# Fourier mixing and a gated feed-forward on one core: a new order of loads and weight conversions ahead of the first chunk

## The chip, the cores and the metric

The kernel runs on one core of one Trainium2 chip. The metric is the device time of one launch in microseconds. The kernel before takes 2041.99 us, the median of 8 runs (2037.69 to 2045.06). One more execution was recorded by the profiler: 2041.35 us, of which the recorded span is 2039.6 us.

## What is computed

Eight sequences x of 3008 rows and 256 features go through a two-dimensional Fourier transform of which the real part is kept, and the result through a gated feed-forward with 1536 inner features. Cut to what matters, the reference is:

```
X = np.fft.fft(x, axis=1)                 # x: (8, 3008, 256) float32
X = np.fft.fft(X, axis=2).real            # 24064 rows of 256
gate = 1 / (1 + exp(-(X @ w_gate)))       # w_gate, w_val: 256 x 1536
out  = (gate * (X @ w_val)) @ w_out       # w_out: 1536 x 256
```

The three weights arrive as 64-bit floats, and the kernel itself turns them into 32-bit ones.

## The kernel before, in words

**Sequence transform.** A batch of x is loaded into the tile x4 as 126 partitions x 4 groups x 6 rows x 256 features: for each row number s it holds the rows s, -s, M+s and M-s, with M = 1504. `fold_ops` (L218) adds and subtracts these groups in place: `point` and `first` (L222 to L227) add a row and its mirror image, `across` (L235) adds or subtracts rows half a sequence apart, and `feat` (L229) folds features j and 256-j. TensorE then multiplies the folded x with tables of cosines and sines (tile st, 126 x 2 x 6 x 753). `half` (L271) makes one such group: its `sums` are six matmuls, one for each of the six rows q, each written into PSUM bank ev or od and each shown in the trace as two pieces of 376 or 377 columns; its `then` evacuates them, with a ScalarE copy (L283) and two VectorE operations (L287, L290). A batch has six groups: four with cosines, into pk and ek, and two with sines, into qk.

**Feed-forward.** The feature transform is merged into the gate and value weights: `weight_use` calls `merge` (L190), eight TensorE pieces `ps` from the table dt and a weight piece, two ScalarE copies into G1 and G2 (L197, L198) and two tiny transfers ge<-G (L200). Output weights go to `forms` (L203), which makes seven sums of blocks on ScalarE and GpSimd. The main loop runs over 8 batches x 6 chunks of 256 sequence frequencies x 6 pairs of feature tiles; each pair takes two turns i of the loop at the bottom of the kernel. A turn calls `front` (matmuls pa and pb, then VectorE L350 twice, L353, L354), `gate` for the turn before (VectorE L365, GpSimd L367 or L369 to L371), from the fifth turn on `back` (the matmuls po), the weight steps in `pre`, the sigmoid (ScalarE L573), and whatever stands in `side` for that turn.

**Weights.** There are 18 pieces, numbered j in `jobs` (L124), each 128 x 2 x 256 values of 8 bytes, 512 KB. Piece j goes through `weight_load` (L130, a transfer on SP's queue), `weight_parts` (L161, two ScalarE operations, L166 and L167), `weight_join` (L169, three VectorE operations L176, L177, L179 and one GpSimd addition L181) and `weight_use`. A piece that is loaded before the main loop lands in buffers that later serve other ends (z, pk, qk, ek, c7); pieces from `KEEP` on use the tile mega, which stands where x4 of batch 0 stood and so is loaded when the sine matmuls have read x4.

**What sets the order.** The schedule is written by hand: each engine executes its instructions in the order in which the code issues them, and loads go through SP's queue in program order. Before the main loop (L469 to L508) that order is:

- SP's queue: three times (a third of x, a third of the cosine table), weights 0 and 1, the sine table in thirds, weights 2 to 7, and after the sine sums weights 8 to 10. dt is issued by ScalarE.
- fold of batch 0 in three parts of two q each; after each part two rows q of all four cosine groups.
- conversions 0 and 1 between the cosine evacuations; merges 0 and 1 between the sine sums; conversions 2 and 3 ahead of the sine evacuations, 4 after them.

In the loop `weight_step` (L520) spreads conversions 5 to 17 over the turns: first one and then two, alternately. Batches 1 to 7 of x are loaded by the same `load_x` during the batch before.

Of the kernel before, what the change touches and what calls it, by code (L numbers as in the profile page):

```python
# [7 lines left out]
F32 = mybir.dt.float32  # L8
# [37 lines left out]
def kernel(  # L46
# [53 lines left out]

    X = {}

    def load_x(b, nq):
        X[b] = xp.tile([NP, 4, NQ, D], F32, name="x4", tag="x4")
        return [lambda q=q: nc.sync.dma_start(out=X[b][:, :, q : q + nq], in_=xf[b, :, :, q : q + nq])
                for q in range(0, NQ, nq)]

    dt = const.tile([P, 2, D], F32, name="dt")
    st = const.tile([NP, 2, NQ, NE + NO], F32, name="st")
# [6 lines left out]
    ed = dram.tile([B - 1, NK], F32, name="ed")  # L116

    def load_table(t, nq):
        return [lambda q=q: nc.sync.dma_start(out=st[:, t, q : q + nq], in_=stab[:, t, q : q + nq])
                for q in range(0, NQ, nq)]  # L120

    jobs = [(w, c - (w == 2)) for c in range(NPR + 1) for w in range(3)  # L124
            if (c if w == 2 else c < NPR)]
    RAW, WS = {}, {}
    mega = []
    KEEP = 8

    def weight_load(j):  # L130


        w, c = jobs[j]
        src = (moe_w_gate, moe_w_val, moe_w_out)[w]
        src = src[2 * c * P : 2 * (c + 1) * P, :] if w == 2 else src[:, c * WC : (c + 1) * WC]
        src = src.rearrange("(c p) f -> p c f", p=P)
        if j < 6:
            if j < 3:
                raw = zp.tile([P, 2, WC, 2], I32, name="raw", tag="z")
            else:  # L140
                raw = pqp.tile([P, 2, WC, 2], I32, name="raw", tag=("pk", "qk", "ek")[j - 3])
            ws = (app if j < 3 else hp).tile([P, 2, WC], F32, name="ws", tag="ae" if j < 3 else "h")
        else:
            if j < KEEP:
                both = cp.tile([P, 3, 2 * WC], F32, name="both", tag="c7")
                r, i = 0, 2
            else:
                if not mega:
                    mega.append(xp.tile([P, 12, 2 * WC], F32, name="mega", tag="x4"))
                both, r, i = mega[0], (j - KEEP) % 3 * 2, 6 + (j - KEEP) % 6  # L150
            raw = both[:, r : r + 2].rearrange("p a n -> p (a n)").bitcast(I32).rearrange(
                "p (c f w) -> p c f w", c=2, w=2)
            ws = both[:, i].rearrange("p (c f) -> p c f", c=2)
        WS[j] = ws
        if src.dtype == F32:
            nc.sync.dma_start(out=ws, in_=src)
        else:
            RAW[j] = raw
            nc.sync.dma_start(out=raw.rearrange("p c f w -> p c (f w)"), in_=src.bitcast(I32))

    def weight_parts(j):  # L161

        if j in RAW:
            raw, ws = RAW[j], WS[j]
            lo, hi = raw[:, :, :, 0], raw[:, :, :, 1]
            nc.scalar.activation(ws, hi.bitcast(F32), AF.Abs)  # L166
            nc.scalar.activation(lo, lo.bitcast(U32), AF.Copy, scale=2.0 ** -29)  # L167
# [50 lines left out]
    def fold_ops(b, nq):  # L218
        x4 = X.pop(b)
        ops = []  # L220

        def point(e, i, j, q):  # L222
            e.tensor_tensor(x4[:, i, q, 1:D], x4[:, i, q, 1:D], x4[:, j, q, D - 1 : 0 : -1],  # L223
                            op=ALU.add)

        def first(e, i, j, q):
            e.tensor_tensor(x4[:, i, q, 0], x4[:, i, q, 0], x4[:, j, q, 0], op=ALU.add)  # L227

        def feat(e, v, r, q):  # L229
            e.memset(r[:, q, 0:1], 0.0)  # L230
            e.tensor_tensor(r[:, q, 1:HD], v[:, q, 1:HD], v[:, q, D - 1 : HD : -1],  # L231
                            op=ALU.subtract)
            e.tensor_tensor(v[:, q, 1:HD], v[:, q, 1:HD], v[:, q, D - 1 : HD : -1], op=ALU.add)  # L233

        def across(e, blk, q):  # L235
            e.tensor_tensor(parts[blk][0][:, q], x4[:, 0, q], x4[:, 2, q],
                            op=(ALU.add, ALU.subtract)[blk])

        parts = [(x4[:, 1], x4[:, 3]), (x4[:, 0], x4[:, 2])]
        qs = [slice(q, q + nq) for q in range(0, NQ, nq)]  # L240
        pool = nc.gpsimd
        if b:

            for i in (0, 2):
                ops += [lambda i=i, q=q: point(pool, i, i + 1, q) for q in qs]
                ops.append(lambda i=i: first(pool, i, i + 1, slice(0, NQ)))
            for blk in range(2):
                ops += [lambda blk=blk, q=q: across(pool, blk, q) for q in qs]
            for v, r in parts:
                ops += [lambda v=v, r=r, q=q: feat(pool, v, r, q) for q in qs]  # L250
        else:

            def part(q, es):
                for e, i in zip(es, (0, 2)):
                    point(e, i, i + 1, q)
                    first(e, i, i + 1, q)
                across(es[0], 0, q)
                feat(es[0], *parts[0], q)
                across(es[1], 1, q)
                feat(es[1], *parts[1], q)  # L260
            for n, q in enumerate(qs):
                ops.append(lambda q=q, es=(nc.vector, pool if n else nc.vector): part(q, es))
        for blk, (v, r) in enumerate(parts):
            W[b, blk] = (v[:, :, 0:HD], r[:, :, 0:HD],
                         v[:, :, HD : HD + 1].to_broadcast([NP, NQ, P]))
        return ops
# [31 lines left out]
    def seq_start(b):  # L298
        PQE[b] = (pqp.tile([P, NK], F32, name="pk", tag="pk"),
                  pqp.tile([P, NK], F32, name="qk", tag="qk"),  # L300
                  pqp.tile([P, NK], F32, name="ek", tag="ek"))
        if b:
            nc.sync.dma_start(out=PQE[b][2], in_=ed[b - 1 : b, :].to_broadcast([P, NK]))
# [163 lines left out]


    nc.scalar.dma_start(out=dt, in_=dtab.rearrange("(c p) d -> p c d", p=P))  # L469
    for fx, ft in zip(load_x(0, 2), load_table(0, 2)):  # L470
        fx()
        ft()
    for j in range(2):
        weight_load(j)
    for f in load_table(1, 2):
        f()
    for j in range(2, KEEP):
        weight_load(j)
    seq_start(0)
    cos = [seq_group(0, blk, what, (2 * blk, 2 * blk + 1) if what else None)  # L480
           for blk in range(2) for what in (0, 2)]
    for i, f in enumerate(fold_ops(0, 2)):
        f()
        for sums, _ in cos:
            sums(2 * i, 2 * i + 1)
    weight_parts(0)
    cos[0][1]()()
    weight_parts(1)
    weight_join(0)
    cos[1][1]()()  # L490
    cos[2][1]()()
    weight_join(1)
    cos[3][1]()()
    sin = [seq_group(0, blk, 1) for blk in range(2)]
    for i in range(NQ // 2):
        for sums, _ in sin:
            sums(2 * i, 2 * i + 1)
        if i < 2:
            weight_use(i, i)
    for j in range(2, 4):  # L500
        weight_parts(j)
        weight_join(j)
    for _, then in sin:
        then()()
    weight_parts(4)
    weight_join(4)
    for j in range(KEEP, KEEP + 3):
        weight_load(j)  # L508

    per = 2 * NPR * len(chunks)  # L510
    side = {}

    def at(i, *fs):
        side.setdefault(i, []).extend(fs)
# [2 lines left out]

        at(i, lambda: at(i + 1, f(*args)))

    def weight_step(i, *js):  # L520

        for j in js:
            pre.setdefault(i, []).append(lambda j=j: weight_parts(j))
            at(i, lambda j=j: weight_join(j))
            if KEEP <= j < len(jobs) - 3:
                at(i, lambda j=j: weight_load(j + 3))

    pre = {}
    for c in range(1, NPR + 1):
        i, j = 2 * c - 3, 3 * c - 1  # L530
        if c < NPR:
            at(max(i, 0), lambda j=j: weight_use(j))
            at(i + 1, lambda j=j: weight_use(j + 1))
            at(i + 2, lambda j=j: weight_use(j + 2))
        else:
            at(i, lambda j=j: weight_use(j))
        if c == NPR:
            weight_step(i - 1, j)
        elif c > 1:
            weight_step(i - 1, j)  # L540
            weight_step(i, j + 1, j + 2)
    i0 = 2 * NPR
    at(i0 + 1, lambda: [f() for f in load_x(1, 3)], e_load)

    for b in range(B - 1):
        s0 = b * per
        if b:
            at(s0 + 1, lambda b=b: [f() for f in load_x(b + 1, 3)])
        f0, g0, gs = (s0 + 9, s0 + 36, 8) if b else (i0 + 9, i0 + 36, 7)

        def folds(f0=f0, b=b):
            for j, f in enumerate(fold_ops(b + 1, 2)):
                at(f0 + j, f)
        at(f0 - 1, folds)
        at(g0 - 3, lambda b=b: seq_start(b + 1))
        for j in range(4):
            split(g0 + gs * j, lambda b=b, j=j: whole(*seq_group(b + 1, j // 2, j % 2)))
# [78 lines left out]
```

## Time and profile before

| What | Value |
|---|---|
| median of 8 runs | 2041.99 us |
| the profiled execution, its own time | 2041.35 us |
| its span | 2039.6 us |
| TensorE busy (matmul) | 2000.3 us, 98% |
| VectorE busy | 1752.2 us, 86% |
| GpSimd busy | 1334.7 us, 65% |
| ScalarE busy | 498.7 us, 24% |
| transfer engines, mean | 35 GB/s |

How to read it: times in the trace count from the span's start. A row of the timeline gives start, duration, engine, line, operation, out<-in, shape, and in brackets how long the engine was idle before it and what released it. A row of the stages gives the length of the stretch, the busy time of each engine with its number of instructions, the granted clock of TensorE (1.00 is full), the busy share of the 16 transfer engines and what they moved. "SPq" is the queue that SP issues transfers on. The first turn of the main loop stands at about 50 us: its first pa matmul starts at 49.76 us.

### The profile page before, as it was taken

The numbers are of one execution on the slowest core, as the hardware profiler recorded it, in microseconds if no ns is written. First come the engines' busy times: TensorE is split into PE (matmuls) and PEld (weight loads), VectorE is DVE, ScalarE is ACT, GpSimd is POOL, SyncE is SP. The second block draws the span as 40 slices with busy tenths as digits, with TensorE's granted clock in tenths as the row PEclk, the third lists the DMA queues.
The fourth block names the chain that finished last, engine by engine and source line by source line (L and its number), as shares of the span: only waits on it lengthen the run. The fifth ranks groups of instructions, "written<-read, shape, count | busy, mean of one in ns | idle before, by whom it ended". The sixth has DMA issues, their size and how long they took to land.

```text
span 2039.6 us, 27360 instructions
## 1 busy us (share of the span) xinstructions
PE 2000.3 (98%) x9168; PEld 1740.7 (85%) x9168; DVE 1752.2 (86%) x3228; ACT 498.7 (24%) x875; POOL 1334.7 (65%) x1681
## 2 busy tenths in 40 slices
PE   6899999999999999999999999999999999999998
PEld 3688789888898889988898888988889888898888
DVE  4999778988799878998789988899878988798887
ACT  2522222222222222222222222222222222222222
POOL 2678645885569755697557955589446885565665
PEclk9899999999999999999999999999999999999999
DMA  9240002010021000200012000201002010000001
GB/s 250 84 73 20 27 11 72 15 31 11 11 77 30 11 11 11 81 26 11 11 23 69 26 12 20 72 10 31 16 11 72 15 31 11 11 16 16 11 16 26
DMA packets 143162, 70.98 MB, mean 35 GB/s; under 512 B 127931, under 2 KB 128187, under 8 KB 143022
## 3 DMA queue, kind: packets, MB, share of 16 engines
q1 hardware_dynamic: 141200, 68.69, 13.0%
q8 instruction: 74, 1.21, 0.2%
q10 hardware_dynamic: 1822, 0.54, 0.1%
q14 instruction: 66, 0.54, 0.1%
HBM read 44.50 MB, written 24.68 MB: 34 GB/s over the span
## 4 chain that ended last, share of the span: by engine, by line
PE 84%; DVE 8%; POOL 4%; DMA 1%; issue 1%; SPq 1%; ACT 0%; DVEq 0%; ACTq 0%; POOLq 0%
PE po L93 37%; PE pa L93 21%; PE pb L93 20%; PE ev L93 3%; PE od L93 3%; DVE ae L350 2%; DVE h L365 2%; DVE z L354 1%; DMA st<-in_stab_dram 1%; DVE z L353 1%; POOL x L233 1%; POOL x L231 1%; POOL sf L370 1%; POOL sf L369 1%; DVE os L412 0%
## 5 line engine op out<-in xcount | busy, mean ns | idle before, releaser
L573 ACT ACTIVATE z<-z 128x512 f32<-128x512 f32 (+1 forms) x576 | 358.5, 622 | 1309.8 <-DVE z L354 1309.8
L350 DVE SCALAR_TENSOR_TENSOR ae<-ek,ge,pa 128x256 f32<-128x256 f32 (+1 forms) x1152 | 489.5, 466 | 189.0 <-PE pa L93 185.1
L93 PE MATMUL pa<-pk,G 128*128 128x256 f32 (+1 forms) x2304 | 583.3, 376 | 2.3 <-ACT a L283 2.3
L93 PE MATMUL pb<-qk,G 128*128 128x256 f32 (+1 forms) x2304 | 582.3, 375 | 1.4 <-DVE qk L287 1.4
L93 PE MATMUL po<-sf,wf 128*128 128x256 f32 (+1 forms) x2304 | 537.2, 375 | 0.8
L93 PEld LDWEIGHTS pa<-pk,G 128*128 128x128 f32 x2304 | 438.5, 190 | 60.1 <-ACT a L283 2.9
L93 PEld LDWEIGHTS po<-sf,wf 128*128 128x128 f32 x2304 | 436.2, 190 | 55.7 <-POOL sf L371 4.5
L93 PEld LDWEIGHTS pb<-qk,G 128*128 128x128 f32 x2304 | 438.2, 190 | 51.9 <-DVE qk L287 2.1
L369 POOL TENSOR_TENSOR sf<-h 128x256 f32<-128x256 f32 (+1 forms) x288 | 213.2, 740 | 391.9 <-DVE h L365 391.9
L365 DVE TENSOR_TENSOR h<-z 128x512 f32<-128x512 f32 (+1 forms) x576 | 451.6, 784 | 0.0
L353 DVE TENSOR_TENSOR z<-ae,pb 128x512 f32<-128x512 f32 (+1 forms) x576 | 390.1, 677 | 62.4 <-DVE ae L350 3.2
L93 PE MATMUL po<-h,wf 128*128 128x256 f32 (+1 forms) x1728 | 412.5, 375 | 0.0
L354 DVE TENSOR_TENSOR z<-ae,pb 128x512 f32<-128x512 f32 (+1 forms) x576 | 386.0, 670 | 0.0
L93 PEld LDWEIGHTS po<-h,wf 128*128 128x128 f32 x1728 | 328.3, 190 | 37.1
L367 POOL TENSOR_TENSOR sf<-h 128x256 f32<-128x256 f32 (+1 forms) x288 | 219.2, 761 | 213.0 <-DVE h L365 209.3
L370 POOL TENSOR_TENSOR sf<-sf,h 128x256 f32<-128x256 f32 (+1 forms) x288 | 215.3, 747 | 22.6
L371 POOL TENSOR_TENSOR sf<-h,sf 128x256 f32<-128x256 f32 (+1 forms) x288 | 214.6, 745 | 22.6
L93 PE MATMUL ev<-st,x 126*128 126x377 f32 (+3 forms) x216 | 78.2, 488 | 17.5 <-DMA st<-in_stab_dram 13.6
L452 ACT COPY c<-po 128x512 f32<-128x512 f32 (+1 forms) x141 | 76.9, 580 | 64.0 <-PE po L93 63.9
L412 DVE STREAM_TRANSPOSE os<-c 128x256 f32<-128x256 f32 x192 | 83.9, 437 | 0.2
L93 PE MATMUL od<-st,x 126*128 126x377 f32 (+3 forms) x216 | 77.5, 485 | 0.0
L223 POOL TENSOR_TENSOR x<-x 126x510 f32<-126x510 f32 x44 | 63.0, 1432 | 19.7 <-DMA x<-in_xf_dram 19.7
(83 smaller groups left out, 727.3 us busy)
## 6 DMA issues: line engine op xcount, KB each, us to landing
x<-in_xf_dram SPq DMA_DIRECT2D x14, 1512.0 KB
out_dram<-os SPq DMA_DIRECT2D x288, 64.0 KB
ek<-ed SPq DMA_DIRECT2D x7, 752.5 KB
out_dram<-os SPq DMA_DIRECT2D x92, 56.0 KB
st<-in_stab_dram SPq DMA_DIRECT2D x6, 741.2 KB
x<-in_xf_dram SPq DMA_DIRECT2D x3, 1008.0 KB
mega<-in_moe_w_out_dram SPq DMA_DIRECT2D x4, 512.0 KB
raw<-in_moe_w_gate_dram SPq DMA_DIRECT2D x3, 512.0 KB
```

The lines of the kernel that those rows point to most:

```text
L93: nc.tensor.matmul(o, l, r, start=start, stop=stop, skip_group_check=True)
L350: nc.vector.scalar_tensor_tensor(out=ae[:, g], in0=ek[:, ks], scalar=ge[:, g, f : f + 1], in1=pa[:, g], op0=ALU.mult, op1=ALU.add)
L353: nc.vector.tensor_tensor(z[:, :, 0], ae, pb, op=ALU.add)
L354: nc.vector.tensor_tensor(z[:, :, 1, ::-1], ae, pb, op=ALU.subtract)
L365: nc.vector.tensor_tensor(h[:, fh], z[:, 0], z[:, 1], op=ALU.mult)
L367: tt(s[:, 2], h[:, 0, 0], h[:, 0, 1], op=ALU.subtract)
L369: tt(s[:, 0], h[:, 0, 1], h[:, 1, 1], op=ALU.add)
L370: tt(s[:, 1], s[:, 0], h[:, 0, 0], op=ALU.subtract)
L371: tt(s[:, 3], h[:, 1, 0], s[:, 1], op=ALU.subtract)
L412: nc.vector.transpose(os_[:, s, 0:nb, h, :], t[:, slot, 0 : nb * TB])
L452: nc.scalar.copy(t[:, 2 * j : 2 * j + 2, 0:n], PO[j][:, :, 0:n])
L573: nc.scalar.activation(z[:, 0], z[:, 0], AF.Sigmoid)
```

## The change

- `load_x` loads a batch as two transfers, groups 0 and 1 and then groups 2 and 3, each with all six rows (12 KB in a row per partition), for every batch. Before, batch 0 came in thirds (2 KB in a row) and the others in halves by q (3 KB in a row).
- The cosine table comes in two transfers (9 KB in a row), the sine table in one (18 KB in a row).
- SP's order becomes: weights 0 and 1, x, cosine table, weights 2 to 5, sine table, weights 6 to 9; after the sine sums weights 10 to 12. `KEEP` is 10, so two more pieces are loaded before the loop, in the buffers os and sf.
- Conversions and merges 0 and 1 stand ahead of everything else on ScalarE, VectorE, GpSimd and TensorE.
- Batch 0 is folded in two parts of three q. VectorE adds groups 0 and 1 for both, GpSimd adds groups 2 and 3 for the second; then `half1` is all on VectorE and `half2` on VectorE and GpSimd. After each part three rows q of all four cosine groups follow; then both sine groups.
- All evacuations stand behind these sums in the code: conversions 2 to 4 ahead of the first, 5 ahead of the second, 6 and 7 ahead of the first sine evacuation, 8 ahead of the last. Merge 2 stands directly ahead of the loop.
- In the loop turn i converts piece i+9 (turns 0 to 8, one each) and the uses follow at fixed turns.

The diff, cut to its core:

```
-    def load_x(b, nq):
-        return [lambda q=q: nc.sync.dma_start(out=X[b][:, :, q : q + nq], in_=xf[b, :, :, q : q + nq])
-                for q in range(0, NQ, nq)]
+    def load_x(b):
+        for h in range(0, 4, 2):
+            nc.sync.dma_start(out=X[b][:, h : h + 2], in_=xf[b, :, h : h + 2])
...
-    KEEP = 8
+    KEEP = 10
...
+            def half1(q):
+                point(nc.vector, 2, 3, q)
+                first(nc.vector, 2, 3, q)
+                for blk in range(2):
+                    across(nc.vector, blk, q)
+                    feat(nc.vector, *parts[blk], q)
+            def half2(q):
+                across(nc.vector, 0, q)
+                feat(nc.vector, *parts[0], q)
+                across(pool, 1, q)
+                feat(pool, *parts[1], q)
+            for q in qs:
+                point(nc.vector, 0, 1, q)
+            first(nc.vector, 0, 1, slice(0, NQ))
+            point(pool, 2, 3, qs[1])
+            first(pool, 2, 3, qs[1])
+            ops += [lambda: half1(qs[0]), lambda: half2(qs[1])]
...
     for j in range(2):
         weight_load(j)
-    for f in load_table(1, 2):
-        f()
-    for j in range(2, KEEP):
-        weight_load(j)
+    load_x(0)
+    load_table(0, NQ // 2)
+    for j in range(2, 6):
+        weight_load(j)
+    load_table(1, NQ)
+    for j in range(6, KEEP):
+        weight_load(j)
...
+    weight_parts(0)
+    weight_parts(1)
+    weight_join(0)
+    weight_join(1)
+    weight_use(0)
+    weight_use(1)
     seq_start(0)
...
-    for i, f in enumerate(fold_ops(0, 2)):
+    for i, f in enumerate(fold_ops(0, NQ // 2)):
         f()
         for sums, _ in cos:
-            sums(2 * i, 2 * i + 1)
+            sums(*range(i * NQ // 2, (i + 1) * NQ // 2))
...
+    for sums, _ in sin:
+        sums(*range(NQ))
+    evacuate = [then for _, then in cos + sin]
+    for then, js in zip(evacuate, ((2, 3, 4), (5,), (), (), (6, 7), (8,))):
+        weight_round(*js)
         then()()
...
     for j in range(KEEP, KEEP + 3):
         weight_load(j)
+    weight_use(2)
...
     pre = {}
+    for j in range(9, len(jobs)):
+        pre.setdefault(j - 9, []).append(lambda j=j: weight_parts(j))
+        at(j - 9, lambda j=j: weight_join(j))
+        if KEEP <= j < len(jobs) - 3:
+            at(j - 9, lambda j=j: weight_load(j + 3))
+    for j in range(3, len(jobs)):
+        w, c = jobs[j]
+        at(2 * c + (-3, -2, 1)[w], lambda j=j: weight_use(j))
```

`weight_round(*js)` calls `weight_parts` and `weight_join` for each j.

More of the change, by code (lines that the diff above doesn't have):

```diff
@@ L118, in load_table @@
     def load_table(t, nq):
-        return [lambda q=q: nc.sync.dma_start(out=st[:, t, q : q + nq], in_=stab[:, t, q : q + nq])
-                for q in range(0, NQ, nq)]
+        for q in range(0, NQ, nq):
+            nc.sync.dma_start(out=st[:, t, q : q + nq], in_=stab[:, t, q : q + nq])
     jobs = [(w, c - (w == 2)) for c in range(NPR + 1) for w in range(3)
@@ L126 @@
     RAW, WS = {}, {}
-    mega = []
-    KEEP = 8
+    shared = {}
+    KEEP = 10
     def weight_load(j):
@@ L136, in weight_load, with some @@
         src = src.rearrange("(c p) f -> p c f", p=P)
-        if j < 6:
-            if j < 3:
-                raw = zp.tile([P, 2, WC, 2], I32, name="raw", tag="z")
-            else:
-                raw = pqp.tile([P, 2, WC, 2], I32, name="raw", tag=("pk", "qk", "ek")[j - 3])
-            ws = (app if j < 3 else hp).tile([P, 2, WC], F32, name="ws", tag="ae" if j < 3 else "h")
-        else:
[L144 to L150, printed above, removed]
+        def some(n, pool, tag):
+            key = tag, (j - 6) // 3 if tag == "c7" else 0
+            if key not in shared:
+                shared[key] = pool.tile([P, n, 2 * WC], F32, name=f"w{tag}", tag=tag)
+            return shared[key]
+        if j < KEEP:
+            pool, tag = ((zp, "z"), (pqp, ("pk", "qk", "ek")[j % 3]), (op, "os"), (sp, "sf"))[
+                j // 3 if j < 6 else j // 2 - 1]
+            raw = pool.tile([P, 2, WC, 2], I32, name="raw", tag=tag)
+            if j < 6:
+                pool, tag = ((app, "ae"), (hp, "h"))[j // 3]
+                ws = pool.tile([P, 2, WC], F32, name="ws", tag=tag)
+            else:
+                ws = some(3, cp, "c7")[:, (j - 6) % 3].rearrange("p (c f) -> p c f", c=2)
+        else:
+            both = some(12, xp, "x4")
+            r, i = (j - KEEP) % 3 * 2, 6 + (j - KEEP) % 6
             raw = both[:, r : r + 2].rearrange("p a n -> p (a n)").bitcast(I32).rearrange(
@@ L251, in fold_ops @@
         else:
[L253 to L262, printed above, removed]
+            def half1(q):
[15 more added lines that the diff above has]
+            ops += [lambda: half1(qs[0]), lambda: half2(qs[1])]
         for blk, (v, r) in enumerate(parts):
@@ L469, with weight_round @@
     nc.scalar.dma_start(out=dt, in_=dtab.rearrange("(c p) d -> p c d", p=P))
-    for fx, ft in zip(load_x(0, 2), load_table(0, 2)):
-        fx()
-        ft()
     for j in range(2):
         weight_load(j)
-    for f in load_table(1, 2):
-        f()
-    for j in range(2, KEEP):
+    load_x(0)
+    load_table(0, NQ // 2)
+    for j in range(2, 6):
         weight_load(j)
+    load_table(1, NQ)
+    for j in range(6, KEEP):
+        weight_load(j)
+    def weight_round(*js):
+        for j in js:
+            weight_parts(j)
+            weight_join(j)
+    weight_parts(0)
[4 more added lines that the diff above has]
+    weight_use(1)
     seq_start(0)
@@ L481 @@
            for blk in range(2) for what in (0, 2)]
-    for i, f in enumerate(fold_ops(0, 2)):
+    for i, f in enumerate(fold_ops(0, NQ // 2)):
         f()
         for sums, _ in cos:
-            sums(2 * i, 2 * i + 1)
[L486 to L493, printed above, removed]
-    sin = [seq_group(0, blk, 1) for blk in range(2)]
[L495 to L503, printed above, removed]
+            sums(*range(i * NQ // 2, (i + 1) * NQ // 2))
+    sin = [seq_group(0, blk, 1) for blk in range(2)]
+    for sums, _ in sin:
[3 more added lines that the diff above has]
+        weight_round(*js)
         then()()
-    weight_parts(4)
-    weight_join(4)
     for j in range(KEEP, KEEP + 3):
         weight_load(j)
+    weight_use(2)
     per = 2 * NPR * len(chunks)
@@ L518, in split @@
         at(i, lambda: at(i + 1, f(*args)))
[L520 to L526, printed above, removed]
-    pre = {}
[L529 to L541, printed above, removed]
+    pre = {}
+    for j in range(9, len(jobs)):
[6 more added lines that the diff above has]
+        at(2 * c + (-3, -2, 1)[w], lambda j=j: weight_use(j))
     i0 = 2 * NPR
-    at(i0 + 1, lambda: [f() for f in load_x(1, 3)], e_load)
+    at(i0 + 1, lambda: load_x(1), e_load)
     for b in range(B - 1):
@@ L547 @@
         if b:
-            at(s0 + 1, lambda b=b: [f() for f in load_x(b + 1, 3)])
+            at(s0 + 1, lambda b=b: load_x(b + 1))
         f0, g0, gs = (s0 + 9, s0 + 36, 8) if b else (i0 + 9, i0 + 36, 7)
```

## The prediction

> **What bounds the kernel now.** I read the page first, then the busy times by stage, then the timeline of TensorE and of VectorE at the end of the ramp, then the first rows that wait for loads.
>
> ```profile
> span 2039.6 us, 27360 instructions
> ...
> PE 2000.3 (98%) x9168; PEld 1740.7 (85%) x9168; DVE 1752.2 (86%) x3228; ACT 498.7 (24%) x875; POOL 1334.7 (65%) x1681
> ...
> PE   6899999999999999999999999999999999999998
> ```
>
> TensorE is at 90% or more in 37 slices, and short only in the first two and the last. By stage:
>
> ```profile
> core 0: us, PE busy (x) PEld busy (x) DVE busy (x) ACT busy (x) POOL busy (x), PEclk, DMA share, GB/s
> 0.00:13.25 13.25, 0.00 (x1) 0.03 (x1) 3.31 (x9) 1.28 (x1) 0.20 (x4) 1.00 0.79 220
> 13.25:49.76 36.51, 29.99 (x88) 17.68 (x88) 18.36 (x35) 8.09 (x18) 12.77 (x15) 1.00 0.94 257
> 49.76:80.00 30.24, 24.34 (x86) 19.27 (x86) 26.67 (x46) 17.05 (x36) 18.40 (x20) 0.78 0.20 64
> 80.00:110.00 30.00, 24.56 (x109) 20.37 (x110) 29.00 (x47) 14.59 (x31) 25.32 (x28) 1.00 0.36 106
> 110.00:130.00 20.00, 20.00 (x95) 17.60 (x94) 18.41 (x34) 5.18 (x12) 14.23 (x21) 1.00 0.47 150
> ```
>
> TensorE idles 13.3 + 6.5 + 5.9 + 5.4 = 31 us before 110, and from there on it is full. So the end is set by when TensorE becomes full and how far it has then come; all that the change can move lies in the first 110 us. Until 49.76 the transfers bind (share 0.79 to 0.94), from 80 to 110 VectorE does (29.0 of 30.0): weight conversions stand on its queue beside the loop's own work. The last idle time, and what follows it:
>
> ```profile
> 106.36 1.99 PE L93 MATMUL ps<-mega,dt 128*128 128x256 f32 x8 [1.19 <-POOL mega L181]
> 108.19 1.03 PE L93 MATMUL pa<-pk,G 128*128 128x256 f32 x4
> 109.06 1.03 PE L93 MATMUL pb<-qk,G 128*128 128x256 f32 x4
> ```
>
> The pb matmul at 109.06 belongs to turn 9, counted from 0, and nothing holds TensorE after it. I use it as the mark: the gain is how much earlier it starts, since the matmuls behind it are the same.
>
> **A turn of the ramp, now and then.** VectorE's ae (L350) of turn 0 starts at 55.09 and that of turn 9 at 110.37, 55.3 us later, with thirteen conversions between. From turn 3 (73.80) to turn 9 it takes 36.57 us for six turns and nine conversions. A turn without a conversion takes 2.8 us (110.37 to 113.14), so a conversion costs (36.57 - 6 x 2.8) / 9 = 2.2 us, a turn with one 5.0. The rows of turn 8, where the conversion's third operation took 1.10 us, give 5.28:
>
> ```profile
> 105.09 0.86 DVE L350 SCALAR_TENSOR_TENSOR ae<-ek,ge,pa 128x256 f32<-128x256 f32 x2
> ...
> 110.37 0.86 DVE L350 SCALAR_TENSOR_TENSOR ae<-ek,ge,pa 128x256 f32<-128x256 f32 x2
> ```
>
> After the change conversions 9 to 17 stand one in each of turns 0 to 8. The mark needs the PSUM bank that ae of turn 8 frees, so it starts 8 x 5.0 - 0.6 (turn 0 has no L365) + 0.9 (that ae) = 40.3 us after ae of turn 0. With 5.28 it is 42.2; I take 5.0, a mean of six turns. TensorE has no more than that to do: nine turns at 1.73 (pa and pb), nine merges at 1.73, backs in turns 4 to 8 of 7.3, together 38.5 us. GpSimd was busy 41.7 of the 55.3 us and loses four additions of 1.4. Both stay under VectorE, though TensorE needs 5.0 of each 5.0 us from turn 4 on.
>
> **The loads.** Where engines first wait shows when they land:
>
> ```profile
> 9.85 0.69 DVE L223 TENSOR_TENSOR x<-x 126x510 f32<-126x510 f32 x1 [9.85 <-DMA x<-in_xf_dram]
> 13.25 0.97 PE L93 MATMUL ev<-st,x 126*128 126x377 f32 x1 [13.25 <-DMA st<-in_stab_dram]
> 18.14 0.69 DVE L223 TENSOR_TENSOR x<-x 126x510 f32<-126x510 f32 x1 [3.70 <-DMA x<-in_xf_dram]
> 25.96 0.69 DVE L223 TENSOR_TENSOR x<-x 126x510 f32<-126x510 f32 x1 [3.27 <-DMA x<-in_xf_dram]
> 36.20 0.56 PE L93 MATMUL ev<-st,x 126*128 126x377 f32 x1 [0.31 <-DMA st<-in_stab_dram]
> ```
>
> A third of x with a third of a table (1.79 MB) takes 8.05 us, 222 GB/s: about 4.85 for x (211 GB/s, 2 KB in a row) and 3.2 for the table (237, 6 KB). dt and the first third of x (1.29 MB) at 222 would need 5.8 of the 9.85 us, so 4.0 are fixed: issue, first bytes, last bytes.
>
> What longer rows are worth isn't shown here. In the Trainium skill, "DMA: Bandwidth & Descriptors", section Specifications, a transfer reaches line rate from pieces of 512 B on; 2 KB are beyond that, so by this rule x stays at 211 GB/s and needs 14.7 us. The rows differ: x of batch 1, 3 KB in a row, crossed while the stretch from 120.0 to 130.5 moved 287 GB/s. That stretch has no table beside it, so the stage may matter as well as the length. Ends for x: 211 to 287; I take 270, 5.7 us for each half, nearer the row of the same tensor. Tables stay at the 237 of 6 KB (9 and 18 KB are only longer), the sine table at the 262 GB/s of the stretch 25.96 to 36.20. A weight piece (0.52 MB) takes 1.8 us at the 292 GB/s of the stretch 36.2 to 48.
>
> Landing in the new order: dt 1.2 and weight 0 at 7.0, weight 1 at 8.8, x at 14.5 and 20.2, cosines at 25.0 and 29.8, weights 2 to 5 at 31.6, 33.4, 35.2, 37.0, sines at 45.7, weights 6 to 9 at 47.5, 49.3, 51.1, 52.9. The four weights cost the sine table 7.2 us; that is the price of this order on SP's queue.
>
> **The work up to turn 0.**
> - Conversions and merges 0, 1: at 7 to 16, on engines that wait for x; cost nothing. Their cover is the 11 us until x.
> - Fold: x at 20.2, then GpSimd's `point` over three rows, 1.77 x 1.5 = 2.65; VectorE's small `first` ended only with it at 18.74 (1.23 us instead of 0.15), so I let it wait again. Then `across` 1.03 and `feat` 1.3: first matmul at 25.4. `half2` ends near 32 on GpSimd, before TensorE wants it.
> - Cosines: 48 pieces of 0.317 are 15.2; the first 5.6 us of matmuls in this trace (13.25 to 18.8) ran at half pace, which costs 2.8: end at 43.4.
> - Conversions 2 to 5: landed by 37.0, VectorE needs 1.6 each, done near 39; the cosine evacuations queued behind them wait for the matmuls anyway. Cost nothing, but if weight 4 were late they would hold the banks that the sine groups need.
> - Sines: at 45.7, after 2.3 us of idle TensorE. In the trace 2.26 us of idleness (47.50 to 49.76) stand ahead of a stretch at clock 0.50 until about 55; the 2.51 us ahead of 82.00 do not. The skill, "TensorE: Matmul & The Clock Gate", What's actually happening, asks for an idle window of some 3.4 us, which would keep this gap warm. By the rule 0, by the first row 3.0 us; two rows disagree, so I take 1.5. 24 pieces are 7.6: end at 54.9.
> - Conversions 6 to 8: weight 8 at 51.1, ScalarE 1.3, VectorE behind it done at 53.4: 1.5 us ahead of the last evacuation that is queued behind it on both. If that cover is gone, each us late is a us of the end.
> - Turn 0: merge 2 (1.73) and pa (0.86) follow the sines, while ScalarE (0.5) and VectorE (1.1) evacuate: ae starts at 57.6. It was 55.09.
> - ge transfers: ae of turn 6 waited for one (1.90 us). Now they are issued a turn ahead, but in turns 2 and 4 behind a weight load that waits for GpSimd's addition: 1.4 + 0.5 + 1.2 + 1.9 = 5.0 us, one turn. Between 0 and 2 us; I take 0. Loading x of later batches in two other halves lies under a full TensorE: 0.
>
> The mark comes at 57.6 + 40.3 = 97.9 instead of 109.06: 11.2 us earlier. Span 2039.6 - 11.2 = 2028.4; this execution took 1.75 more than its span, and the median is 0.6 above it: about 2030.
>
> **Rivals.**
> - Longer rows do little: x at 211 (+3.3), the sines start cold (+1.5), perhaps turns of 5.28 (+1.9). Gain 4 to 7, 2035 to 2038. For it: the skill's rule and the tables' 237 GB/s at 6 KB. Against: 287 for x. 0.17.
> - Everything crosses at 287: x ends at 19.5, cosine sums at 42.7, sines land before that, no cold start; sines end near 50.4. Gain 16, about 2026. 0.10.
> - The conversions only move: all unfavourable ends together, with weights landing 2.26 us apart (ScalarE's waits end at 30.65 and 32.91) so that weight 8 holds the last evacuation. Gain about 2, 2040. 0.09.
> - Slower: few long rows, 126 of them to spread over 16 engines, cross worse than short ones, and the sine table, behind four weights, holds turn 0. At 160 GB/s x takes 8.0 more, cosines 4.6, sines 5.5: 18 - 11 = 7 slower, 2048. It decides from 181 GB/s down; the lowest row is 211. 0.08.
>
> **Numbers.** The forecast, 2024 to 2034, has 0.56. About 0.2% (4 us) is what a measurement of this kernel can tell from no change. Faster 0.56 + 0.17 + 0.10 = 0.83, same 0.09, slower 0.08. The range reaches from the faster case into all of the second one: 2022 to 2038.
>
> **What would show it.** Sine matmuls near 45.7, ae of turn 0 near 57.6, turns of 5.0 us with TensorE idle under 1 us in each, the mark near 98, and no idle time after it. Wrong if the sines land after 50, if VectorE waits for a ge transfer or a conversion in turns 1 to 8, or if the clock column shows half pace in turn 0 or later.

## The result, and the profile after

The changed kernel took 2029.18 us (median of 12 runs, 2026.67 to 2032.24), the kernel before beside it 2040.08 us (33 runs, 2034.03 to 2045.91): a ratio of 0.9948, with a 95% interval of 0.9937 to 0.9960. It is 10.9 us faster. The forecast was 2030.0. Beside the later runs the kernel before had medians of 2036.66, 2037.36 and 2040.19 us, so the gain is 7 to 11 us depending on which of them is taken, and ratios from different sets can differ by 0.2% where the times do not.

The page of the changed kernel, its head and the row of TensorE in 40 slices:

```profile
span 2026.9 us, 27347 instructions
...
PE 1995.8 (98%) x9168; PEld 1738.9 (86%) x9168; DVE 1755.2 (87%) x3221; ACT 498.4 (25%) x875; POOL 1328.1 (66%) x1675
...
PE   6999999999999999999999999999999999999998
```

TensorE has the same 9168 matmuls. The second slice has filled, from 8 to 9. The same five stages as before, with the same columns:

```profile
0.00:13.25 13.25, 3.83 (x10) 3.16 (x11) 5.03 (x7) 3.92 (x6) 2.77 (x6) 1.00 0.80 286
13.25:49.76 36.51, 25.76 (x74) 15.04 (x74) 27.42 (x44) 11.92 (x23) 13.74 (x11) 0.86 0.88 257
49.76:80.00 30.24, 28.00 (x126) 23.48 (x125) 27.28 (x48) 16.13 (x35) 18.46 (x22) 1.00 0.33 105
80.00:110.00 30.00, 29.70 (x137) 25.32 (x136) 28.05 (x48) 12.01 (x29) 22.81 (x31) 1.00 0.15 36
110.00:130.00 20.00, 20.00 (x95) 17.60 (x94) 19.27 (x36) 6.12 (x11) 14.44 (x21) 1.00 0.71 157
```

Read the matmul counts: in the third stage 126 instead of 86, in the fourth 137 instead of 109. TensorE's idle time there fell from 5.9 and 5.4 us to 2.2 and 0.3, and no clock below 1.00 is left behind 49.76. The second stage holds fewer matmuls than before (74 for 88), because the first cosine sum now waits for all of x. VectorE does 9 us more there; the conversions taken out of the ramp are among it.

The ends of the ramp, on the timelines of VectorE (ae of turn 0) and TensorE (pb of turn 9, the mark), each row with its start and its duration:

```profile
54.23 0.87 DVE L364 SCALAR_TENSOR_TENSOR ae<-ek,ge,pa 128x256 f32<-128x256 f32 x2 [0.77 <-PE pa L93]
```

```profile
95.17 1.03 PE L93 MATMUL pa<-pk,G 128*128 128x256 f32 x4
96.03 1.03 PE L93 MATMUL pb<-qk,G 128*128 128x256 f32 x4
```

From ae of turn 0 to the mark it takes 41.80 us, where it was 109.06 - 55.09 = 53.97. From the mark to the end it takes 2026.9 - 96.03 = 1930.9, where it was 1930.5. So the gain of this execution, 13.0 us at the mark, is 12.2 in the ramp and 0.9 ahead of it. The medians differ by 1.7 us less than these two executions do (2041.35 and 2028.71), well within the spread of either kernel's runs.

The first rows that wait for loads, on the timelines of VectorE (x) and TensorE (tables):

```profile
12.40 1.82 DVE L229 TENSOR_TENSOR x<-x 126x765 f32<-126x765 f32 x2 [1.57 <-DMA x<-in_xf_dram]
18.55 0.96 DVE L229 TENSOR_TENSOR x<-x 126x765 f32<-126x765 f32 x1 [4.24 <-DMA x<-in_xf_dram]
19.43 1.77 DVE L233 TENSOR_TENSOR x<-x 126x3 f32<-126x3 f32 x1
```

```profile
24.02 2.85 PE L93 MATMUL ev<-st,x 126*128 126x377 f32 x4 [9.27 <-DMA st<-in_stab_dram]
43.77 2.14 PE L93 MATMUL ev<-st,x 126*128 126x377 f32 x6 [1.48 <-DMA st<-in_stab_dram]
```

All of x is in by 18.55, where its last third came at 25.96; the sines begin at 43.77.

### The profile page after: what moved, and what is told of

Same layout as the page of the kernel before. It is cut to its first block, busy times and chain, and to the rows that moved or that the text cites. A ratio compares the mean times of both kernels' runs of the same rounds, so it can differ in the third digit from the quotient of the medians.

```text
span 2026.9 us, 27347 instructions
## 1 busy us (share of the span) xinstructions
PE 1995.8 (98%) x9168; PEld 1738.9 (86%) x9168; DVE 1755.2 (87%) x3221; ACT 498.4 (25%) x875; POOL 1328.1 (66%) x1675
## 4 chain that ended last, share of the span: by engine, by line
PE 85%; DVE 7%; POOL 4%; DMA 2%; issue 1%; ACT 0%; DVEq 0%; SPq 0%; ACTq 0%; POOLq 0%
PE po L93 37%; PE pa L93 21%; PE pb L93 21%; PE ev L93 3%; PE od L93 3%; DVE ae L364 2%; DVE h L379 2%; DVE z L368 1%; DMA ge<-G 1%; DVE z L367 1%; POOL x L239 1%; POOL x L237 1%; DMA st<-in_stab_dram 1%; POOL sf L384 1%; POOL sf L383 1%
## 5 line engine op out<-in xcount | busy, mean ns | idle before, releaser
L471 POOL TENSOR_TENSOR c<-c 128x512 f32<-128x512 f32 (+1 forms) x47 | 73.6, 1565 | 0.0
```

## The experiments

The theory: the gain is made in the ramp, by the four conversions that VectorE no longer does there, and the loads only keep turn 0 where it was. The first rival: the gain comes from the longer rows. The second: what is left ahead of turn 0 is a stall that the new order made. "Mark" and "ramp" are meant as above, and every ratio is to the kernel before.

**Conversions back in the loop.** Conversions 5, 6 and 7 go back into the turns, everything else stays as changed.

```diff
-    ... ((2, 3, 4), (5,), (), (), (6, 7), (8,))):
+    ... ((2, 3, 4), (), (), (), (), (8,))):
...
-    for j in range(9, len(jobs)):
-        pre.setdefault(j - 9, []).append(lambda j=j: weight_parts(j))
+    turn = {5: 0, 6: 1, 7: 1, 9: 2, 10: 3, 11: 4, 12: 5, 13: 5, 14: 6, 15: 7, 16: 7, 17: 8}
+    for j in turn:
+        pre.setdefault(turn[j], []).append(lambda j=j: weight_parts(j))
...
```

> The changed kernel, but conversions 5, 6 and 7 stand in the loop again (turns 0 and 1, the later ones then two in some turns), all loads as changed. If the gain lies in the conversions taken out of the ramp: three more at 2.2 us on VectorE, less up to 1.8 us of ge waits that they would cover, so turn 9's pb starts at 101 to 103 instead of 96.0 and the time is 2034 to 2036. If it lies in the loads: ae of turn 0 near 54 and the time within 1 us of 2029.

Measured: 2035.42 us, ratio 0.9986 (0.9976 to 0.9995), 6.2 us more than the changed kernel and than the next run, which stood beside it. The ramp of this kernel by stage, and that of the changed one:

```profile
50.96:100.33 49.37, 41.29 (x179) 34.21 (x178) 47.68 (x77) 26.92 (x58) 33.08 (x39) 0.97 0.27 79
```

```profile
54.23:96.03 41.80, 39.25 (x179) 33.23 (x177) 38.48 (x66) 22.75 (x51) 26.56 (x33) 1.00 0.31 93
```

Each has 179 matmuls. VectorE works 9.2 us longer in the ramp of this kernel and is busy in 47.68 of 49.37 us; the ramp is 7.6 us longer, 2.5 us for each conversion put back. TensorE's longest wait in it is for a converted weight:

```profile
80.13 3.46 PE L93 MATMUL ps<-wx,dt 128*128 128x256 f32 x8 [4.23 <-POOL wx L187]
```

Ahead of turn 0 they show no cost: from the first sine sum to ae of turn 0 it takes 10.46 us here (40.50 to 50.96, conversion 8 alone in it) and 10.46 in the changed kernel (43.77 to 54.23, conversions 6 to 8 in it). Conversion 5 stands ahead of the sine sums, which in both wait for their table.

The conversions are the larger part of the gain. A fourth at the same price makes 10.1 of the 12.2 us. In the ramp before, VectorE also stood idle twice, in turn 1 for a conversion's addition on GpSimd and in turn 3 for TensorE, which then ran at half pace (granted clock 0.52 from 68.4 to 73.6):

```profile
60.30 0.87 DVE L350 SCALAR_TENSOR_TENSOR ae<-ek,ge,pa 128x256 f32<-128x256 f32 x2 [1.41 <-POOL ws L181]
...
73.80 0.87 DVE L350 SCALAR_TENSOR_TENSOR ae<-ek,ge,pa 128x256 f32<-128x256 f32 x2 [1.23 <-PE pa L93]
```

The changed kernel has neither wait. Together they are 2.6 us, about what is left of the gain, with 1.8 us of new waits for ge against it; no run takes them away alone.

**Short rows for x.** x of batch 0 crosses in the new halves, but each in three transfers of 2 KB rows.

```diff
-            nc.sync.dma_start(out=X[b][:, h : h + 2], in_=xf[b, :, h : h + 2])
+            n = NQ if b else 2
+            for q in range(0, NQ, n):
+                nc.sync.dma_start(out=X[b][:, h : h + 2, q : q + n],
+                                  in_=xf[b, :, h : h + 2, q : q + n])
```

> The changed kernel, but each half of batch 0's x comes in three transfers with 2 KB in a row instead of one with 12 KB. If longer rows cross faster: 7.3 us for a half instead of 6.15 (211 GB/s against 252), x at 14 and 21, the sines 2 us later, 2031. If 2 KB are beyond what matters[...]: x at 12.4 and 18.6 as in the changed kernel, 2029.

Measured: 2029.2 us, ratio 0.9953 (0.9935 to 0.9971), no different from the changed kernel. The halves of x were in by 12.26 and 17.36 (where GpSimd, which needs the last of the three transfers, starts), not later than in 12 KB rows (12.40 and 18.55), and the ramp took 41.73. The length of x's rows shows no cost here.

**The cosine and sine tables in thirds.** Both tables in transfers of 6 KB rows, as before, instead of 9 and 18 KB.

```diff
-    load_table(0, NQ // 2)
+    load_table(0, 2)
-    load_table(1, NQ)
+    load_table(1, 2)
```

> The changed kernel, but both tables come in thirds with 6 KB in a row instead of 9 and 18 KB. If longer rows make the tables faster (before moved them at 237 GB/s): first cosine matmul 2 to 3 us later, sines 3 us later, 2032. If the length does not matter: cosines at 22 to 24, sines at 40 to 44 as in the other runs, 2029.

Measured: 2026.2 us, ratio 0.9939 (0.9916 to 0.9962), not slower either. First cosine sum at 23.72. The sines began earlier, at 40.81, on the first third, but then TensorE waited 2.01 us for the next one and ran its first groups at half pace (granted clock 0.56 from 44.3 to 45.6):

```profile
40.81 1.52 PE L93 MATMUL ev<-st,x 126*128 126x377 f32 x4
44.34 1.55 PE L93 MATMUL ev<-st,x 126*128 126x377 f32 x2 [2.01 <-DMA st<-in_stab_dram]
45.68 3.15 PE L93 MATMUL od<-st,x 126*128 126x377 f32 x6
```

This profiled execution took 2029.68 us, the longest of the four; the others took 2024.41 to 2027.37.

**Halves of x and of the table in turns.** Long rows, but the first half of the cosine table stands between the halves of x.

```diff
-    load_x(0)
-    load_table(0, NQ // 2)
+    for h in (0, 2):
+        load_x(0, (h,))
+        load_table(0, NQ // 2, range(3 * h // 2, 3 * h // 2 + 3))
...
```

> The changed kernel, but the two halves of x and the two cosine parts alternate on SP's queue as they did before, long rows kept. If it is the alternation that made x slow before: x's second half and the end of the cosine table come together near 25 to 28 instead of 18.6 and 24, sines 2 us later, 2031. If order alone counts: the second half at 22.5, the first cosine matmul near 27, and the sines at 40 to 44 with the cosine sums at 45 as the bound: 2031 too, but with the weights 2 to 4 landing as before.

Measured: 2029.9 us, ratio 0.9961 (0.9949 to 0.9973). x was in at 12.57 and 22.66, the first cosine sum ran at 27.52, the sines at 44.26 without a wait: now the cosine sums and not the table bound their start. The order alone costs 0.7 us of median, less than the runs can tell.

**The loads as before.** x and the cosine table of batch 0 in the six short transfers of before, in their order, behind weights 0 and 1. The conversions stay as changed.

```diff
-    load_x(0)
-    load_table(0, NQ // 2)
+    load_both()
...
+    def load_both():
+        X[0] = xp.tile([NP, 4, NQ, D], F32, name="x4", tag="x4")
+        for q in range(0, NQ, 2):
+            nc.sync.dma_start(out=X[0][:, :, q : q + 2], in_=xf[0, :, :, q : q + 2])
+            nc.sync.dma_start(out=st[:, 0, q : q + 2], in_=stab[:, 0, q : q + 2])
```

> The changed kernel, but batch 0's x and the cosine table come in the six short-rowed, alternating transfers of the kernel before, behind weights 0 and 1 (the sine table stays one transfer). If it is short rows and alternation together that made those loads slow (222 GB/s): the last third of x at 27 to 29 instead of 16 to 20, the first cosine matmul after 31, sines later than 45, 2032 or more. If the loads cross no slower: the last third near 21 to 23 (what lies ahead of it is 1.5 MB more), and 2029 to 2031.

Measured: 2032.47 us, ratio 0.9965 (0.9953 to 0.9976): 3.3 us of the gain gone. x was complete at 26.54, the first cosine sum at 32.34, ae of turn 0 at 59.60, and the ramp took 41.77. Its loads, by stretches, and those of the changed kernel:

```profile
18.00:25.00 7.00, 0.00 (x0) 0.00 (x0) 0.95 (x1) 0.00 (x0) 0.00 (x0) 0.54 1.02 252
25.00:30.00 5.00, 0.00 (x0) 0.00 (x0) 3.46 (x4) 0.00 (x0) 3.42 (x2) 0.50 1.04 224
```

```profile
8.00:12.00 4.00, 2.58 (x6) 2.14 (x7) 2.64 (x3) 0.66 (x2) 2.31 (x2) 1.00 0.86 313
12.00:18.00 6.00, 2.75 (x11) 1.98 (x10) 1.91 (x3) 1.29 (x4) 0.25 (x1) 1.00 0.95 298
18.00:24.00 6.00, 0.00 (x0) 0.01 (x1) 5.36 (x7) 0.00 (x0) 2.73 (x2) 0.63 0.94 254
```

With the transfers of before two thirds of the table, 1.5 MB, cross ahead of the last of x, and at a DMA share of 1.02 to 1.04 only 224 to 252 GB/s are moved. With the changed order x has nothing but weights 0 and 1 beside it and crosses at 298 to 313. At 298 GB/s these 1.5 MB alone would be 5 of the 8 us by which x came later. So with the conversions as changed the arrangement of the loads is worth about 3 us by the medians; within it, neither the row length of x nor that of the table nor the order shows a cost of its own. What makes the rate low is not settled, and it is not bound to the old arrangement: in the run with later ge transfers, below, with long rows in the changed order and weights 2 to 4 already queued behind x, 8 to 12 us moved 241 GB/s at a share of 1.04.

**ge on ScalarE's queue.** All transfers of ge are issued by ScalarE, none by SP.

```diff
-            (nc.sync if c else nc.scalar).dma_start(
+            nc.scalar.dma_start(
```

> The changed kernel, but all ge transfers are issued on ScalarE's queue, none on SP's behind weight loads. If the queue makes them late: VectorE's waits for ge in turns 5 and 7 (1.26 and 0.58 us) are gone, turn 9's pb starts near 94.2, 2027.4. If the tiny transfers themselves are slow, or ScalarE's issuing (two at 0.6 us per merge) holds its sigmoids: the waits stay or move to L575, 2029 to 2031.

Measured: 2027.03 us, ratio 0.9945 (0.9929 to 0.9962). In the changed kernel VectorE waited for ge in two turns:

```profile
74.73 0.48 DVE L364 SCALAR_TENSOR_TENSOR ae<-ek,ge,pa 128x256 f32<-128x256 f32 x1 [1.26 <-DMA ge<-G]
...
85.23 0.48 DVE L364 SCALAR_TENSOR_TENSOR ae<-ek,ge,pa 128x256 f32<-128x256 f32 x1 [0.58 <-DMA ge<-G]
```

Here neither wait is left, and the ramp took 40.26 instead of 41.80. That is 1.5 of the 2.2 us by which the mark came earlier; the median moved by as much, inside what the runs can tell.

**The first ge transfers later.** The chain of waits of the changed kernel (start, duration, what) runs through an unexpected step:

```profile
14.04 14.99 DMA ge<-G
...
29.05 0.37 SPq L165
...
29.46 14.17 DMA st<-in_stab_dram
```

The ge transfers of merges 0 and 1, four of 0.5 KB, take up to 15 us to land while x and the cosine table cross in long rows (9.12 and 12.00 us in the chains of two other runs), and SP's next issue waits for their end; the sine table stands behind it. Here they are issued only after the fourth cosine evacuation.

```diff
+        if c:
+            ge_load(g, c)
...
+        if then is evacuate[3]:
+            ge_load(0, 0)
+            ge_load(1, 0)
```

> The changed kernel, but the ge transfers of merges 0 and 1 are issued on ScalarE's queue after the fourth cosine evacuation instead of at 13.5 and 15.2 us. If SP stood until 29.05 only because of them: the sine table is issued near 20 to 25 and lands 2 to 4 us earlier, at 40 to 42; the sine matmuls then follow the cosines at once (42.3), ae of turn 0 at 52.5 to 53, 2027.5. If the bytes bind: sines at 43.8, time within 0.5 us of the changed kernel.

Measured: 2028.32 us, ratio 0.9952 (0.9937 to 0.9968): 0.9 us less than the changed kernel, inside what the runs can tell. The stall is gone, SP issued the sine table at 15.99. SP's earlier issues moved too (weight 2 from 12.40 to 3.93); whether the chip or the program's own semaphores tie SP to these transfers is not shown. But the sine sums started at 43.27, and no longer waited for the table:

```profile
43.27 2.14 PE L93 MATMUL ev<-st,x 126*128 126x377 f32 x6 [1.17 <-ACT a L301]
```

ScalarE's evacuation, which frees the bank, had itself waited 2.43 us for VectorE's, which stands behind conversions 2 to 5. So the stall of SP was largely covered by work that ends nearly as late. All of x came 1.5 us later in this execution (20.06); counted from the first cosine sum, the sine sums began 18.35 us after it, where it was 19.75, so the stall was worth 1.4 us at most in this pair.

**No conversions in the loop.** VectorE's operations of conversions 9 to 17 are left out.

```diff
+        if j >= 9:
+            nc.gpsimd.tensor_tensor(wi, wi, lo, op=ALU.add)
+            return
```

> The changed kernel with part of the computation left out: of conversions 9 to 17 VectorE's three operations are not done (those weights stay raw). If VectorE is what holds the ramp: a turn falls from 5.0 to 2.8 us on VectorE and TensorE becomes the bound, 38.5 us from pa of turn 0 to the end of merge 15, so turn 9's pb starts 3 to 4 us earlier than 96.0, and moving still more conversions ahead is worth no more than that: 2025 to 2026. If the ge transfers or GpSimd hold it: 95 to 96, 2029.

Measured: 2028.05 us, ratio 0.9949 (0.9929 to 0.9969). The ramp took 39.84, only 2.0 less. VectorE's ae now waited for ge where it used to convert, 8.5 us instead of 1.8:

```profile
72.19 0.48 DVE L367 SCALAR_TENSOR_TENSOR ae<-ek,ge,pa 128x256 f32<-128x256 f32 x1 [4.58 <-DMA ge<-G]
82.59 0.48 DVE L367 SCALAR_TENSOR_TENSOR ae<-ek,ge,pa 128x256 f32<-128x256 f32 x1 [3.90 <-DMA ge<-G]
```

These waits are VectorE's, and count only as far as TensorE waits with it. The next run takes both away: the same with ge on ScalarE's queue.

> The changed kernel with all ge transfers on ScalarE's queue, and with part of the computation left out: of conversions 9 to 17 VectorE's three operations are not done. If the ge waits took the place of VectorE in the run that only left these out (turn 9's pb 39.8 us after ae of turn 0): now TensorE alone binds, 38.2 us after, and the conversions that are left in the loop cost 2 us. If something else holds the ramp: 39.8 again.

Measured: 2026.37 us, ratio 0.9932 (0.9906 to 0.9957). The ramp took 38.22; VectorE's ae waits in it for TensorE alone. That is TensorE's own time: it is busy in all of it. Of the changed kernel's 41.80, 1.5 are ge waits, 2.0 conversions that TensorE still waits for, and 38.2 TensorE. The two costs simply add up (3.6 together), and the 8.5 us of waits were worth 1.6.

**The changed kernel again.** No edit.

> The changed kernel once more, on the same chip as the others of this call, to see how far its loads vary: x between 11 and 14.5 us, sines between 40 and 44, ae of turn 0 between 51 and 55, and turn 9's pb 41.8 us after that whatever the loads do.

Measured: 2030.17 us, ratio 0.9957 (0.9940 to 0.9974). x came at 11.95 and 17.95, the ramp took 41.76. But TensorE was idle for longer ahead of the sines and then ran its first six groups in 3.68 instead of 2.14 us (granted clock 0.58 from 43.7 to 47.4, where it was 1.00 in the first execution):

```profile
43.71 3.68 PE L93 MATMUL ev<-st,x 126*128 126x377 f32 x6 [3.72 <-DMA st<-in_stab_dram]
```

The mark came at 97.47, 1.4 later than in the first execution, by this alone.

**Both remedies.** ge on ScalarE's queue, and the tables in thirds; the edits are those above.

> The changed kernel with all ge transfers on ScalarE's queue and both tables in thirds. If the two act apart: no ge waits (1.8 us) and TensorE starts the sines on the first third instead of idling 1.5 to 3.9 us ahead of them: turn 9's pb 40.3 us after ae of turn 0, the sines begun before 42, 2025 to 2026. If the thirds bring nothing of their own: 2027, as with ge on ScalarE alone.

Measured: 2023.25 us (6 runs, 2022.93 to 2024.93), ratio 0.9920 (0.9903 to 0.9938). It beats both kernels: its slowest run lies 0.8 us below the fastest of all runs of the changed one (2025.73, in the repeat). The start of its sine sums:

```profile
38.23 1.43 PE L93 MATMUL ev<-st,x 126*128 126x377 f32 x4
40.43 0.90 PE L93 MATMUL ev<-st,x 126*128 126x377 f32 x2 [0.77 <-DMA st<-in_stab_dram]
```

They begin straight behind the cosines (38.23 where it was 43.77), wait 0.77 us for the second third and keep the full clock (1.00 from 38.2 to 48). The ae of turn 0 starts at 50.04, the ramp takes 40.24, the mark comes at 90.28. Not all of this is the edit: x was in at 16.32 and the first cosine sum ran at 21.18, 2.8 us earlier than in the changed kernel. The fair neighbour is the run with ge on ScalarE alone, with x at 16.43 and the first cosine sum at 21.30. It had one transfer for the whole sine table, 3.17 us of idle time ahead of it and then half pace, and reached ae of turn 0 at 53.56, 3.5 us later. With thirds alone the wait was 2.01 us and cost the clock, but that was the longest of its four executions, and the ge transfers that moved are first issued behind the sine sums, so they cannot have made the difference there. By the medians the remedies add up: 3.0 us for the thirds, 2.2 for ge, 5.9 for both.

## Why the prediction was right, step by step

**The mark decides: right.** From the mark to the end all thirteen profiled executions need 1930.2 to 1931.5 us. What moved lies ahead of it.

**VectorE's conversions bind the ramp: right, by experiment.** The prediction had 2.2 us for each and a ramp of 40.3 us; the conversions put back cost 2.5 each, and the ramp is 41.80. TensorE's own 38.5 us came out as 38.22, so the nine conversions that are left bind by 2.0 us only. The turn of 5.0 was a mean that held by some luck: with ge on ScalarE turns 0 and 1 took 3.70 and 4.75 us and the others 5.1 to 5.2, together 39.34 to ae of turn 8, where 8 x 5.0 - 0.6 is 39.4. With 5.28 the prediction's own sum gives 42.5, not 42.2.

**ge "between 0 and 2 us; I take 0": the size was off.** They cost 1.26 + 0.58 = 1.8 us as waits, in turns 4 and 6 counted from 0, and 1.5 us of the ramp when removed. Without them the ramp was 40.26 us. A wait for ge in turns 1 to 8 was one of the prediction's own signs of being wrong, and for this step it is: the bound held and the value within it did not. The working had a full turn of queueing for a lead of one turn, so there was nothing to spare. The 1.90 us that it took for a wait of turn 6 were the transfer's own time in the chain of waits; VectorE stood idle for ge in no turn of the ramp before.

**The loads: right in size, wrong in reason.** For x 5.7 us were taken for each half; measured are 6.2 (12.40 to 18.55), 6.0 in the repeat and 5.2 with ge on ScalarE. The reason, longer rows, fell: 2 KB rows in the same order were no slower (x in at 17.36 against 18.55). The Trainium skill's rule ("DMA: Bandwidth & Descriptors", Specifications: line rate from 512 B on), which was weighed and set aside, agrees with that run; it doesn't explain why the arrangement of before moved 232 to 242 GB/s at the same place. The prediction read 211 against 287 as an effect of the rows, when order and neighbours differed as well. Weights 0 and 1 were 1.4 us earlier than worked out (5.63 and 7.43), so the 4.0 us of fixed time were too many, and everything behind was 1.4 to 2.1 us early.

**Fold and cosines: right.** VectorE's small `first` did wait for GpSimd and took 1.77 us; the cosine sums ran from 24.02 to 42.3, 18.3 us where 15.2 + 2.8 was the sum.

**The sine table behind four weights: the right time on another path.** 45.7 was worked out, 43.77 measured. What held its issue was not the bytes of the weights alone but the ge transfers that SP's queue waited for; with that gone VectorE's conversions and evacuations held the sines to 43.27.

**The cold start, 1.5 us: not in the first execution, in full in the second.** After 1.48 us of idle time the clock stayed, after 3.72 us it fell and cost 3.68 - 2.14 = 1.5 us. The rule that the prediction weighed against its first row, by which such a gap costs nothing, does not come out of these runs: 2.01 us were followed by half pace, with the tables in thirds. From the sines to ae of turn 0 it was 54.23 - 43.77 = 10.5 us; 7.6 + 2.7 had been worked out.

**The sum.** Turn 0 came 3.4 us earlier than forecast (1.9 the sines, 1.5 the clock), the ramp was 1.5 us longer: mark 96.03 for 97.9. Two misses partly cancel, which is luck. The last line of the prediction's sum, 2028.4 + 1.75 + 0.6, gives 2030.8 rather than 2030; the median was 2029.18. The rival in which longer rows do little was right on the rows and wrong on the gain, since it took x at 211 GB/s for that. The slower rival, with few long rows below 181 GB/s, never came near: x itself crossed at 298 to 313, and in stretches of 3 to 5 us from 20 to 43 us the changed kernel's loads moved no less than 207 GB/s.

**Open.** Executions whose loads stand in the order of the changed kernel have x complete between 16.23 and 20.06 us and ae of turn 0 between 50.96 and 56.69, and that is not explained. The ae of turn 0 of before is known from one execution, so the 0.9 us ahead of turn 0 is too.

## What to carry to other kernels

When one engine is full from some point on, find that point and ask only how early it comes; here a conversion moved out of a ramp that VectorE bound, into a stretch where it waited, was worth 2.5 us of the ramp and 2.1 by the medians, about all of its time. A small transfer has to be placed by what is queued ahead of it on its way, not by its size, and its lead is to be worked out in turns of the loop. A wait that stands in a trace is not its price: 8.5 us of waits on VectorE were worth 1.6, because TensorE waited with it for no longer. And where single executions differ by some us, compare the ones whose loads came at the same time before you give an edit the credit.

## What the runs showed of the hardware

- Transfers of 0.5 KB took 15.0 us to land (9.1 and 12.0 in two other runs) beside rows of 9 to 12 KB on another queue, and an issue on SP waited for their end (29.05).
- How much idle time costs TensorE its clock was not one number: 1.48, 1.70 and 1.99 us (conversions back) did not, 2.01 us did (tables in thirds), as did 3.17, 3.72 and 3.9 us; before the change 2.26 us stood ahead of half pace and 2.51 us did not.
- At a DMA share of 0.93 to 1.04 the core's transfers moved from 224 GB/s (loads as before, 25 to 30 us, 1.04) to 315 (short rows, 12 to 16 us, 0.93), so the share does not tell the rate.
